# Block 0 of a fused attention and MLP kernel: when weight conversions may enter the engine queues

## Chip, cores and metric

One Trainium2 chip, one of its cores. The metric is the device time of one execution in microseconds (us). Engines: PE is TensorE, DVE VectorE, ACT ScalarE, POOL GpSimd, SP SyncE, whose queue issues all DMAs here.

## What is computed

Attention of 8 heads over 576 positions for 4 batches (4 heads see the last 32 positions, 4 heads every 32nd), then a gated layer with an RMS norm, then a second one without. All in fp32.

```python
attn_out = _attn_ref(q, k, v)                       # (4, 8, 576, 64)
x = attn_out.transpose(0, 2, 1, 3).reshape(2304, 512)
rms = np.sqrt(np.mean(x * x, axis=-1, keepdims=True) + 1e-06)
xn = x / rms * rms_g
g = xn @ w_gate                                     # 512 x 1536
x = (g * (1.0 / (1.0 + np.exp(-g))) * (xn @ w_val)) @ w_out
a, b = x @ w_a, x @ w_b
out = (a * b) @ w_out2                              # (2304, 512)
```

## The kernel before

The 2304 tokens go through the first layer in 6 blocks of 384 columns (`t`), and the hidden width of 1536 in 12 chunks of 128 (`fc`). Every fp32 operand of a product is split into a high and a low fp32r part, `hi` and `lo = x - hi`, and a product is three matmuls (`mm3`: hi·hi, hi·lo, lo·hi). For a chunk PE makes `g_ps` and `v_ps` (12 matmuls each), then `y` (12 matmuls, four accumulators that live for the block), one chunk behind. Between them, DVE multiplies `g_ps` by `rinv`, the reciprocal root mean square (line 750), ACT takes silu (751), DVE multiplies by `v_ps` to `h` (761), and `split` makes hi of h on ACT (502) and lo on POOL or DVE (503). Three PSUM slots with the tag "gv" hold g and v, so that g of chunk 2 takes the slot of v of chunk 0.

The weights come as 64-bit words, and block 0 converts them while it computes. The conversion of a third (gate, val, out; for chunks 1 to 10 gate and val go together, 1024 columns, called gv here, and out, called wo, is 512 wide) has these steps: ACT at line 134 turns the high word into a float in place; the low bits go to `cz`, either by ACT from the upper half of the low word (line 139, letter A of `LOW`) or by DVE as a shift of it (line 136, letter D); DVE joins them (line 142); ACT casts hi (147); POOL or DVE subtracts to lo (148, letters of `WLO`). A converted `wo` is also stored to DRAM (`wod`), from which later blocks load it. The raw weights of chunks 0 to 6 and some of `wo` are loaded ahead, the rest as slots become free.

Attention of block 0 runs first (list `STEPS0`); its end for this text is: `pvc` and `xstc` call `xhl` four times, which makes hi of x on ACT (384), the square on ACT (429, inside `sq`, which also issues the matmul with `ones`, 433) and lo on DVE (386). Then `rinv` takes the root on ACT (445) and the reciprocal on DVE (447). Attention of block t + 1 is spread over the chunks of block t (`attention_slot`).

The order of each engine's instructions comes from a planner of the tile framework: among the instructions that its own timeline finds ready it takes the one that was emitted first. The kernel bends this order by `tc.issue_after(i)`: within it, whatever is emitted for i's engine is queued behind i; no other engine is touched and no wait between engines is added. `gate(fc)` does so for the keys in `GATES`, each an instruction of block 0's attention: `snorm`, `sqr`, `pvr` and `rec` are on DVE, `sqrt`, `xhi` and `sexp` on ACT, `pvm` on POOL. `behind(list)` does it for a list; `made` holds h (DVE), hi (ACT) and lo of the latest chunk.

Of the kernel before, what the change touches and what calls it, by code (L numbers as in the profile page):

```python
# [10 lines left out]
F32 = mybir.dt.float32  # L11
# [4 lines left out]
ALU = mybir.AluOpType  # L16
# [9 lines left out]
NFC = FF // 128  # L26
# [17 lines left out]

GATES = ["pvm snorm sqr",
         "norm pvm snorm sqr",
         "pvr snorm xhi",
         "snorm sqr sqrt xhi",
         "rec sexp snorm sqrt xhi"]

# [14 lines left out]
WLO = ["PPP", "PPP", "PPP", "PPP", "PPP", "PPP",  # L65
       "PPP", "PPP", "PPP", "PPP", "PPP", "PPD"]

LOW = ["AAA"] * NFC
NEG = -1000000000.0
BIG = 3.0e38  # L70
SCALE = 1.0 / 8.0
# [3 lines left out]
def fused_kernel(ctx: ExitStack, tc: tile.TileContext, qtl, ktl, vl, qs, ks, vs, cst, w1, w2, out):  # L75
# [5 lines left out]
    nc = tc.nc  # L81

    def engine(c):
        return {"P": nc.gpsimd, "D": nc.vector}[c]
# [29 lines left out]
    def load_pair(w, which, pool=None):  # L114
        if pool is None:
            t = gv_slot(U32, "gv_raw")
            if which[0][1] == 0:
                gvraw[which[0][0]] = t
            return [load_raw(w, fc, k, t[:, i]) for i, (fc, k) in enumerate(which)]
        return [load_raw(w, fc, k, raw_third(pool)) for fc, k in which]  # L120
# [46 lines left out]
    def run(steps):  # L167
        for f in steps:
            f()
# [14 lines left out]
    def attention(t, pool, psum, banks):  # L184
# [4 lines left out]
        st = {}  # L189
        steps = {}  # L190

        def bank():
            return psum.tile([128, 512], F32, tag=next(banks), name="att")

        def piece(tag, name, bufs):
            return pool.tile([128, NTB], F32, tag=tag, name=name, bufs=bufs)
# [183 lines left out]
        def xhl(i, src):  # L380

            xx = act.tile([128, 2, NTB], F32R, tag="x", name="xx", bufs=8)
            hi, lo = xx[:, 0], xx[:, 1]
            st["xhi"] = nc.scalar.activation(hi, src, AF.Copy, scale=g_sb[:, i:i + 1])
            sq(i)()
            st["xlo"] = nc.vector.scalar_tensor_tensor(lo, src, g_sb[:, i:i + 1], hi.bitcast(F32), op0=ALU.mult, op1=ALU.subtract)
            xt[t, i] = xx

        def xsplit(i, src):
# [35 lines left out]
        def sq(i):  # L425
            def f():
                q_t = st["sq", i] = piece("sq", "sq", 2)
                src = st["ops" if i < 2 else "xps", i % 2][:, :NTB]
                nc.scalar.activation(q_t, src, AF.Square)
                if t == 0:  # L430
                    if i == 0:
                        st["rps"] = bank()
                    nc.tensor.matmul(st["rps"][:, :NTB], ones, q_t, start=i == 0, stop=i == 3)
                elif i:
                    engine(SQA[t]).tensor_tensor(q_t, q_t, st["sq", i - 1], op=ALU.add)
            return f
# [50 lines left out]
    def tmp(name):  # L487
        return act.tile([128, NTB], F32, tag="t", name=name, bufs=NTMP)

    made = []  # L490

    @contextmanager
    def behind(instructions):

        with ExitStack() as e:
            for i in instructions:
                e.enter_context(tc.issue_after(i))
            yield
# [17 lines left out]
    g_sb = cst_sb[:, 384:388]  # L516
# [19 lines left out]
    def load_late(which):  # L536
        raw.update(zip(which, load_pair(w1, which, pool)))

    def convert1(fc):
        t = gv[fc] = gv_slot(F32R, "gv")  # L540
        two = [raw.pop((fc, k)) for k in range(2)]
        if fc in FUSEDW:
            both, ready = gvraw[fc], t.rearrange("p k a n -> p (k a) n")
            run(conversion(both.rearrange("p k a n -> p (k a) n"), ready, pool, engine(WLO[fc][0]), LOW[fc][0]))
        else:
            run(zipped(*(conversion(two[k], t[:, k], pool, engine(WLO[fc][k]), LOW[fc][k]) for k in range(2))))

# [29 lines left out]
    @contextmanager  # L577
    def gate(fc):

        with ExitStack() as e:  # L580
            for key in GATES[min(fc, len(GATES) - 1)].split():
                e.enter_context(tc.issue_after(s0["st"][key].ins))
            yield
# [23 lines left out]
    def load_wo(t, fc):  # L607
        wt = wo[t, fc] = wo_tile()
        nc.sync.dma_start(wt.rearrange("p a n -> p (a n)").bitcast(F32), wod[fc])
# [110 lines left out]
    for t in range(NB):  # L720
        if t == 1:
            apool.close()
            pool = apool.enter_context(tc.tile_pool(name="attn", bufs=1))
        if t == NB - 1:
            apool.close()
            cpool.close()
            pool = p2.enter_context(tc.tile_pool(name="forms", bufs=1, reuse_waits="tile"))
            early = [f for k in (4, 5, 0, 1, 2, 3) for f in convert_forms(k, k < 4)]
        nxt = attention(t + 1, pool, psum, itertools.cycle(["att"])) if t + 1 < NB else None
        x = [xt[t, cc] for cc in range(NCC)]  # L730
        for fc in range(NFC):
            if t > 0 and fc == 0:
                load_wo(t, 0)
            g_ps = psum.tile([128, 512], F32, tag="gv", name="g_ps", bufs=3)
            mm_in(g_ps[:, :NTB], gv[fc], 0, x)
            v_ps = psum.tile([128, 512], F32, tag="gv", name="v_ps", bufs=3)
            mm_in(v_ps[:, :NTB], gv[fc], 1, x)
            if t == 0 and fc + 1 < NFC:
                with gate(fc + 1):
                    convert1(fc + 1)  # L740
                if fc + 2 == NFC:
                    load_late([(NFC - 2, 2), (NFC - 1, 2)])
            if t == NB - 1:
                slab[fc] = wgt.tile([128, 4 * DM], F32 if fc in (0, 1, 11) else F32R, tag="gv", name="slab", bufs=NFC)
                with behind(made):
                    run(early[len(early) * fc // NFC:len(early) * (fc + 1) // NFC])
                    for k in [k for k in x0 if k <= fc]:
                        run(x0.pop(k))
            sg = tmp("sg")
            nc.vector.tensor_tensor(sg, g_ps[:, :NTB], ri[t], op=ALU.mult)  # L750
            nc.scalar.activation(sg, sg, AF.Silu)  # L751
            if fc == 1 and t > 0:
                evac_y(t - 1)
            if nxt is not None:
                attention_slot(nxt, fc)
            if prev is not None:
                emit_y(*prev)
            if t > 0 and fc + 1 < NFC:
                load_wo(t, fc + 1)
            h = tmp("h")  # L760
            made[:] = [nc.vector.tensor_tensor(h, sg, v_ps[:, :NTB], op=ALU.mult).ins]  # L761
            hl[t, fc] = split(h, engine(HLO0[fc] if t == 0 else HLO[t]))
            if t == 0:
                wt = wo[0, fc] = wo_tile()
                with gate(fc + 1):
                    run(conversion(raw.pop((fc, 2)), wt, pool, engine(WLO[fc][2]), LOW[fc][2], True))
                nc.sync.dma_start(wod[fc], wt.rearrange("p a n -> p (a n)").bitcast(F32))
                if fc % 2:
                    load_units(1)
                if fc == NFC - 3:  # L770
                    load_late([(NFC - 1, 0), (NFC - 1, 1)])
            prev = (t, fc)
    emit_y(*prev)
    evac_y(NB - 1)
# [238 lines left out]
```

## Time and profile before

| | |
|---|---|
| median of 3 runs | 982.59 us (980.43 to 1163.71) |
| the profiled execution | 981.18 us |
| its span, first to last instruction | 979.4 us |
| mean granted clock of PE | 0.99 |
| instructions | 14348 |

The profile shows one execution. Its times count from the first instruction; the 1.8 us between its time and its span lie outside. The run of 1163.71 stands apart from the other two and from the profiled one, and is not used.

### The profile page before, as it was taken

The page shows a single profiled execution, that of the slowest core. Times are in us where ns is not written, and L with a number is a line of the kernel's source. Part 1 is how long each engine was busy: PE and PEld are TensorE (multiplying, and loading weights), DVE is VectorE, ACT ScalarE, POOL GpSimd, SP SyncE. Part 2 cuts the span into 40 slices and gives each one's busy share as a digit, 9 for nine tenths or more (in the row PEclk, how much of TensorE's full clock was granted, in tenths as well). Part 3 has the DMA queues.
Part 4 walks back from the last instruction along what each step waited for, and adds up shares of the span by engine and source line. Part 5 has one row for each costly group of instructions (what it writes and reads, how often), then busy time and mean ns, then how long its engine had stood idle before and what let it go on. Part 6 is the DMA issues. An engine that isn't in the chain of part 4 may idle for free.

```text
span 979.4 us, 14348 instructions
## 1 busy us (share of the span) xinstructions
PE 944.5 (96%) x5438; PEld 896.9 (92%) x5438; DVE 625.2 (64%) x903; ACT 429.3 (44%) x800; POOL 537.6 (55%) x406
## 2 busy tenths in 40 slices
PE   5799999999999999999998999999999999999998
PEld 4699889999999999999998999899999999999996
DVE  5578757648917885887566657666656655465534
ACT  5989645243534433433455555435335423122110
POOL 4488846558739776968346544755643424123211
PEclk7989999999999999999999999999999999999999
DMA  9953376435534553532687975897893973863701
GB/s 347 407 231 119 114 282 210 147 117 177 187 108 134 200 168 110 173 121 80 213 343 302 344 281 206 318 417 319 337 366 138 356 293 113 284 248 150 269 11 65
DMA packets 57364, 215.57 MB, mean 220 GB/s; under 512 B 5968, under 2 KB 14544, under 8 KB 51664
## 3 DMA queue, kind: packets, MB, share of 16 engines
q1 hardware_dynamic: 57296, 214.66, 59.9%
q8 instruction: 43, 0.70, 0.3%
q14 instruction: 25, 0.20, 0.1%
HBM read 172.17 MB, written 42.47 MB: 219 GB/s over the span
## 4 chain that ended last, share of the span: by engine, by line
PE 69%; DVE 10%; DMA 7%; ACT 6%; POOL 4%; issue 4%; SPq 0%; POOLq 0%; DVEq 0%; ACTq 0%
PE o L892 5%; PE o L894 5%; PE o L893 5%; PE Y L838 4%; PE Y L837 4%; PE Y L836 4%; PE y L478 3%; PE v_ps L478 3%; PE y L479 3%; PE y L480 3%; PE v_ps L480 3%; PE g_ps L478 3%; PE v_ps L479 3%; PE g_ps L480 3%; PE g_ps L479 3%
## 5 line engine op out<-in xcount | busy, mean ns | idle before, releaser
L148 POOL TENSOR_TENSOR hl<-c,hl 128x384 fp32r<-128x384 f32 x72 | 79.8, 1109 | 185.7 <-ACT hl L147 180.1
L245 POOL TENSOR_TENSOR prod<-kv_t,qs_t 128x512 f32<-128x512 f32 (+12 forms) x57 | 107.7, 1913 | 17.8 <-DMA kv_t<-in_ks 5.9
L478 PE MATMUL g_ps<-xx,gv 128*128 128x384 f32 x288 | 98.2, 341 | 5.1 <-DVE h L761 5.1
L843 DVE TENSOR_TENSOR c<-c,Y 128x384 f32<-128x384 f32 x108 | 59.3, 551 | 67.5 <-PE Y L838 59.7
L478 PE MATMUL v_ps<-xx,gv 128*128 128x384 f32 x288 | 97.7, 339 | 2.6 <-DVE sg L750 2.1
L479 PE MATMUL y<-hl,wo 128*128 128x384 f32 x288 | 96.1, 338 | 4.0 <-DVE hl L503 4.0
L479 PE MATMUL v_ps<-xx,gv 128*128 128x384 f32 x288 | 98.1, 341 | 0.0
L278 POOL TENSOR_TENSOR prod<-kv_t,S_t 128x512 f32<-128x512 f32 (+12 forms) x57 | 84.8, 1500 | 23.9 <-issue 7.4
L480 PE MATMUL v_ps<-xx,gv 128*128 128x384 f32 x288 | 97.5, 339 | 0.0
L480 PE MATMUL g_ps<-xx,gv 128*128 128x384 f32 x288 | 97.3, 338 | 0.0
L479 PE MATMUL g_ps<-xx,gv 128*128 128x384 f32 x288 | 97.1, 338 | 0.0
L480 PE MATMUL y<-hl,wo 128*128 128x384 f32 x288 | 94.8, 337 | 0.0
L503 POOL TENSOR_TENSOR hl<-h,hl 128x384 fp32r<-128x384 f32 x58 | 62.8, 1083 | 47.8 <-ACT hl L502 41.3
L281 DVE TENSOR_REDUCE xs_t<-prod 128x64 f32<-128x448 f32 (+17 forms) x57 | 85.2, 1515 | 6.0 <-POOL prod L278 5.8
L478 PE MATMUL y<-hl,wo 128*128 128x384 f32 x288 | 85.6, 343 | 1.1 <-ACT wo L147 0.9
L892 PE MATMUL o<-slab,hl 128*128 128x512 f32 x216 | 84.7, 393 | 1.0 <-DVE slab L901 0.5
L893 PE MATMUL o<-slab,hl 128*128 128x512 f32 x216 | 84.6, 392 | 0.0
L894 PE MATMUL o<-slab,hl 128*128 128x512 f32 x216 | 83.5, 395 | 0.0
L147 ACT CAST hl<-c 128x384 fp32r<-128x384 f32 x72 | 37.0, 513 | 104.1 <-DVE c L873 103.9
L751 ACT ACTIVATE sg<-sg 128x384 f32<-128x384 f32 x72 | 37.9, 526 | 90.9 <-DVE sg L750 80.3
L838 PE MATMUL Y<-slab,form 128*128 128x384 f32 x216 | 73.1, 338 | 0.0
L837 PE MATMUL Y<-slab,form 128*128 128x384 f32 x216 | 73.0, 338 | 0.0
(135 smaller groups left out, 2515.5 us busy)
## 6 DMA issues: line engine op xcount, KB each, us to landing
form<-formd SPq DMA_DIRECT2D x32, 1792.0 KB, 10.7
wo<-wod SPq DMA_DIRECT2D x60, 512.0 KB, 3.5
raw<-in_w SPq DMA_DIRECT2D x42, 512.0 KB, 6.9
gv_raw<-in_w SPq DMA_DIRECT2D x30, 512.0 KB, 10.0
formd<-form SPq DMA_DIRECT2D x6, 1792.0 KB, 6.8
formd<-forms SPq DMA_DIRECT2D x6, 1792.0 KB, 11.8
slab<-x2d SPq DMA_DIRECT2D x24, 384.0 KB, 4.5
wod<-wo SPq DMA_DIRECT2D x12, 512.0 KB, 3.3
```

Of the source, the lines that this page charges most:

```text
L148: lo_eng.tensor_tensor(lo, x, hi.bitcast(F32), op=ALU.subtract)
L245: nc.gpsimd.tensor_tensor(pr, st["ks", g][:, :, :n, :], st["qs"][:, heads(g), mm:mm + 1, :].to_broadcast([128, G, n, D]), op=ALU.mult)
L278: st["pvm"] = nc.gpsimd.tensor_tensor(pr, st["vs", g][:, :, :n, :], st["S"][:, heads(g), mm, :n, None].to_broadcast([128, G, n, D]), op=AL ...
L281: st["pvr"] = nc.vector.tensor_reduce(st["xs"][:, mm, heads(g), :], pr.rearrange("p g n d -> p g d n"), axis=X, op=ALU.add)
L478: nc.tensor.matmul(out_ps, w_hi, x_hi, start=start, stop=False)
L479: nc.tensor.matmul(out_ps, w_hi, x_lo, start=False, stop=False)
L480: nc.tensor.matmul(out_ps, w_lo, x_hi, start=False, stop=stop)
L837: nc.tensor.matmul(bank(n), hi, x[p][:, 1, c], start=False, stop=False, skip_group_check=not begins)
L838: nc.tensor.matmul(bank(n), lo, x[p][:, 0, c], start=False, stop=c == 1, skip_group_check=not begins)
L892: nc.tensor.matmul(o, h[:, 0, cols], w[0], start=n == 0, stop=False)
L893: nc.tensor.matmul(o, h[:, 0, cols], w[1], start=False, stop=False)
L894: nc.tensor.matmul(o, h[:, 1, cols], w[0], start=False, stop=n == len(chunks) - 1)
```

## The change

Four edits, all for block 0. `xhl` emits the lo part ahead of the square. The third entry of `GATES`, which holds for gv of chunk 2 (and for wo of chunk 1), names the root instead of the last reduction of the attention's products: on ACT its instructions queue behind the root, on DVE no longer behind that reduction. `wo` of chunk 0 gets the same gate (`max(fc + 1, 2)`). A list `h_made` keeps h and its two parts for each chunk of block 0; gv of chunk fc + 1 and wo of chunk fc queue, on their three engines, behind those of chunk fc - 2, which takes hold from gv 3 and wo 2 on. And the low bits of gv 1 and gv 2 are made by DVE (line 136) instead of ACT (line 139).

```diff
 GATES = ["pvm snorm sqr",
          "norm pvm snorm sqr",
-         "pvr snorm xhi",
+         "snorm sqr sqrt xhi",
          "snorm sqr sqrt xhi",
          "rec sexp snorm sqrt xhi"]
...
-LOW = ["AAA"] * NFC
+LOW = ["AAA", "DDA", "DDA"] + ["AAA"] * 9
...
             st["xhi"] = nc.scalar.activation(hi, src, AF.Copy, scale=g_sb[:, i:i + 1])
+            st["xlo"] = nc.vector.scalar_tensor_tensor(lo, src, g_sb[:, i:i + 1], hi.bitcast(F32), op0=ALU.mult, op1=ALU.subtract)
             sq(i)()
-            st["xlo"] = nc.vector.scalar_tensor_tensor(lo, src, g_sb[:, i:i + 1], hi.bitcast(F32), op0=ALU.mult, op1=ALU.subtract)
...
+    h_made = {}
     made = []
...
             if t == 0 and fc + 1 < NFC:
-                with gate(fc + 1):
+                with gate(fc + 1), behind(h_made.get(fc - 2, [])):
                     convert1(fc + 1)
...
                 wt = wo[0, fc] = wo_tile()
-                with gate(fc + 1):
+                with gate(max(fc + 1, 2)), behind(h_made.get(fc - 2, [])):
                     run(conversion(raw.pop((fc, 2)), wt, pool, engine(WLO[fc][2]), LOW[fc][2], True))
...
+            if t == 0:
+                h_made[fc] = list(made)
             prev = (t, fc)
```

## Rows read from the trace of the kernel before

**Rows 1.** The page, part 1: busy us, share of the span, instructions.
```profile
PE 944.5 (96%) x5438; PEld 896.9 (92%) x5438; DVE 625.2 (64%) x903; ACT 429.3 (44%) x800; POOL 537.6 (55%) x406
```
**Rows 2.** Stretches: length, busy us (instructions) by engine, PE's clock, DMA share, GB/s.
```profile
33.40:56.20 22.80, 17.10 (x79) 15.92 (x78) 12.16 (x14) 22.30 (x32) 10.61 (x6) 0.85 1.04 407
56.20:126.90 70.70, 67.93 (x432) 63.89 (x430) 56.66 (x68) 56.60 (x111) 61.24 (x40) 1.00 0.38 138
126.90:180.00 53.10, 49.74 (x303) 48.26 (x304) 36.37 (x63) 24.59 (x61) 33.18 (x30) 1.00 0.65 225
180.00:979.40 799.40, 787.38 (x4470) 750.24 (x4468) 502.57 (x720) 304.67 (x554) 416.89 (x316) 1.00 0.59 216
```
**Rows 3.** Waits of PE, 33 to 260 us: us in total, times, longest.
```profile
PE g_ps L478 <- DVE h L761: 5.1, 2, 4.7
```
**Rows 4.** Timeline of PE: start, us, instruction, tiles, count, idle before and releaser.
```profile
33.48 0.42 PE L478 MATMUL g_ps<-xx,gv 128*128 128x384 f32 x1
...
44.29 0.34 PE L480 MATMUL v_ps<-xx,gv 128*128 128x384 f32 x1
49.37 0.69 PE L478 MATMUL g_ps<-xx,gv 128*128 128x384 f32 x1 [4.75 <-DVE h L761]
...
56.23 0.85 PE L478 MATMUL y<-hl,wo 128*128 128x384 f32 x4
56.92 0.34 PE L478 MATMUL g_ps<-xx,gv 128*128 128x384 f32 x1
...
59.00 0.34 PE L478 MATMUL v_ps<-xx,gv 128*128 128x384 f32 x1
```
**Rows 5.** Timeline of ACT, 31 to 49 us.
```profile
31.52 1.16 ACT L134 ACTIVATE gv_raw<-gv_raw 128x1024 f32<-128x1024 f32 x1
32.55 1.15 ACT L139 ACTIVATE cz<-gv_raw 128x1024 uint32<-128x1024 uint16 x1
33.56 0.69 ACT L134 ACTIVATE gv_raw<-gv_raw 128x512 f32<-128x512 f32 x1
...
34.67 0.90 ACT L429 ACTIVATE sq<-att 128x384 f32<-128x384 f32 x2
...
37.50 0.58 ACT L445 ACTIVATE rms_t<-att,eps_sb 128x384 f32<-128x384 f32 x1 [0.47 <-PE att L433]
...
46.91 1.28 ACT L751 ACT_TABLE_LOAD   x1
48.20 0.52 ACT L751 ACTIVATE sg<-sg 128x384 f32<-128x384 f32 x1
```
**Rows 6.** Timeline of DVE, 38 to 49 us.
```profile
38.12 2.55 DVE L447 RECIPROCAL rinv<-rms_t 128x384 f32<-128x384 f32 x1 [1.51 <-ACT rms_t L445]
...
41.66 0.55 DVE L750 TENSOR_TENSOR sg<-g_ps,rinv 128x384 f32<-128x384 f32 x1
42.77 1.23 DVE L142 SCALAR_TENSOR_TENSOR cz<-gv_raw,cz 128x1024 uint32<-128x1024 uint32 x1 [0.56 <-ACT cz L139]
...
48.76 0.56 DVE L761 TENSOR_TENSOR h<-sg,v_ps 128x384 f32<-128x384 f32 x1 [3.62 <-ACT sg L751]
```
**Rows 7.** Timeline of POOL: lo parts of gv 3, wo 2, h 0 and gv 7.
```profile
46.97 2.35 POOL L148 TENSOR_TENSOR gv<-cz,gv 128x1024 fp32r<-128x1024 f32 x1 [6.73 <-ACT gv L147]
...
52.09 1.28 POOL L148 TENSOR_TENSOR wo<-cz,wo 128x512 fp32r<-128x512 f32 x1
53.33 1.02 POOL L503 TENSOR_TENSOR hl<-h,hl 128x384 fp32r<-128x384 f32 x1
...
75.36 2.39 POOL L148 TENSOR_TENSOR gv<-cz,gv 128x1024 fp32r<-128x1024 f32 x1
```
**Rows 8.** Line 343 up to 137 us: duration ns min/median/max, first and last start, forms.
```profile
L343 DVE TENSOR_SCALAR lsm<-lsm x6: 153/658/1329, 11.6 to 80.8; 128x4 f32<-128x4 f32 x4, 64x8 f32<-64x8 f32 x2
```
**Rows 9.** Timeline of ACT: first step of gv 7, and hi of h 4.
```profile
65.70 1.13 ACT L134 ACTIVATE gv_raw<-gv_raw 128x1024 f32<-128x1024 f32 x1
...
80.72 0.50 ACT L502 CAST hl<-h 128x384 fp32r<-128x384 f32 x1
```

## Prediction

> **What bounds the kernel now.** Read the page first: TensorE (PE) is busy for 96% of the span [rows 1], so a change elsewhere pays only where PE stands still or runs slowly. Then the stretches, one row for each: of the 799 us behind 180 us PE is busy for 787, so nothing is to be won there except that all of it starts earlier. Block 0's run-up, 33.4 to 56.2, is the bad one: 17.10 busy of 22.80, at a mean granted clock of 0.85, that is partly at the lower of the two levels (1.2 instead of 2.4 GHz), while ScalarE (ACT) is busy for 22.30 [rows 2]. Third, the waits of PE: of the 5.1 us spent on h (VectorE, line 761), one wait has 4.7 [rows 3]. Fourth, the timelines around that wait. PE issues the last matmul of v_ps 1 at 44.29 and the first of g_ps 2 at 49.37; from there to the end of chunk 2 at 56.23 it needs 6.86 us for 24 matmuls, against 2.08 us for 12 in chunk 3 (59.00 - 56.92), 0.173 us each [rows 4]. PE waits for a PSUM slot: three hold g and v, and g_ps 2 takes that of v_ps 0, which is free after h 0.
>
> Following h 0 back: it ran at 48.76, right behind silu 0 (48.20, after a table load at 46.91), whose input sg was there at 41.66 + 0.55 = 42.21 [rows 5, 6]. So silu 0 stood 6.0 us in ACT's queue behind conversions. The sg itself waited for the reciprocal (38.12, 2.55 us), this for the root at 37.50, this for the last two squares at 34.67, and those stood behind four conversion steps that ACT took from 31.52 on [rows 5, 6]. These are the two queues that the change touches.
>
> **The change, part by part.** *Ahead of the root.* The conversions of gv 2, wo 0 and wo 1 move behind it; the four steps from 31.52 to 34.67 go, 3.15 us [rows 5]. The low bits of gv 1 (one ACT step, as 1.15 us of gv 2) leave ACT as well; some half microsecond of that helps, since the products that feed x 0 bound it next. I take the root 3.6 us earlier, at 33.9 (bounds 3.0 and 5.0). Reciprocal: 34.5 to 37.1. In the kernel before, a conversion step stood between it and sg 0; I keep none, so sg 0 is made at 37.65, 4.6 us earlier, if g_ps 0 is through: 12 matmuls from 33.48 end at 35.6 [rows 4].
>
> *The lo parts ahead of the squares.* VectorE (DVE) and ACT are different engines, so this only lets the four lo parts precede other DVE work; matmuls of g_ps 0 with lo need them. DVE has gaps there; I set it at nothing, bounds -0.6 and +0.6 us.
>
> *Silu 0 and h 0.* Between root and silu 0, ACT may now find only gv 2, wo 0 and wo 1. Their first two steps (1.16 for gv 2; some 0.69 each for four wo steps, by the one at 33.56 [rows 5]) make 3.9 us, a little more than the 3.25 us from the end of the root (34.4) to sg. They end at 38.3; with the table load of 1.28 silu 0 starts near 39.6 and h 0 is done near 40.7 (0.52 and 0.56 us [rows 5, 6]); if the three closing casts (1.1 + 2 x 0.69) slip in front too, near 43.2. Before: 49.3. So 6 to 9 us earlier.
>
> *gv 2 as the next to be late.* Its chain now begins at the root: ACT 34.4 to 35.6; the shift on DVE behind reciprocal and sg, near 37.7. No row shows this shift. Nearest from above is line 142 over the same 1024 words, 1.23 us [rows 6]; from below half of it, 0.6; I take 1.2, the same width on the same engine. Then line 142, 1.23, to 40.1, the cast 1.1, to 41.2, the lo part on GpSimd (POOL) 2.35 [rows 7], to 43.6. PE is done with g 0, v 0, g 1 and v 1 (48 matmuls, 8.3 us) at 41.8, starts g_ps 2 at once and waits for lo parts to about 43. Chunk 2 ends near 47.2 at the full clock, against 56.23: **9 us ahead**. Of that some 6.3 is the earlier start and 2.7 the clock (6.86 - 24 x 0.173).
>
> A wait that the shift adds, first from the row: TENSOR_SCALAR on DVE, line 343, takes 153 ns at best and 1329 ns at worst for the same few elements [rows 8], the long ones beside busy POOL. The Trainium skill, page "SBUF — State Buffer", section "Who interferes with whom", says why it can speak against this change: tensor_scalar in a two-port mode, and an operation with two SBUF inputs, share a port pair with GpSimd as an exclusive lock, so low bits on DVE could block on POOL's instructions where ACT's never do. By that rule the sum would lose up to one POOL conversion, 2.35 us, on gv 2 and nothing on gv 1; by the best row nothing. The trace agrees with the lock. POOL has little to do at 36 to 40, so I leave it at nothing, with 1.2 us in the range.
>
> *Behind the root: the three-chunk rule.* From gv 3 and wo 2 on, each conversion queues on ACT, DVE and POOL behind h, hi and lo of three chunks before (gv) or two (wo). What is queued behind these waits are L134, L139, L142, the casts and POOL's lo parts, and for them wait PE and, on SP's queue, the stores wod<-wo and the loads behind them. The price is the run-ahead: before, ACT converted through gv 6 while PE stood still. Sum it for the stretch from the end of chunk 2 to the start of block 1 (70.7 us, 56.2 to 126.9 [rows 2]). POOL: 61.24 busy, and to it come what was done before 56.2 and now falls behind 47.2: lo parts of gv 3 and gv 4 (2 x 2.35), wo 2 (1.28), h 0 (1.02): 68.2 us [rows 2, 7]. ACT: 56.60, and what is left over: before, it worked 56.2 - 38.0 = 18.2 us without a gap behind the root; now 47.2 - 34.4 = 12.8, of which the moved gv 2 and wo 0, wo 1 take 2.3 + 6 x 0.69 = 6.4; so 11.8 us are left over: 68.4. PE: 67.9. All three need 68 us, so from 47.2 the stretch can't end before 115.6. Before, PE filled 67.93 of 70.70 (96%) and POOL 87%. Three engines that are all full, tied by short waits, will not each reach 96%; I take 91.5%, between the two rows: 68.4 / 0.915 = 74.8, block 1 starts at **122.0 instead of 126.9, 4.9 us earlier**. So 4 of the 9 us are given back. At 96% it is 118.5 (8.4 gained), at 87% 125.8 (1.1 gained).
>
> *Behind 127 us.* Block 2's attention loads queue on SP behind the last wo store, so they move with block 0's conversions; PE stands for 3.4 of 53.1 us there and 12 of 799 afterwards [rows 2], which I keep.
>
> **Sum.** The profiled execution took 981.18 (span 979.4 and 1.8 around it); it lies between the two undisturbed runs shown, 980.43 and 982.59, the latter being the median. 981.2 - 4.9 = 976.3, so **976**.
>
> **Rivals.** *Absorbed (980).* The wait on h 0 turns into the same time lost later, since ACT and POOL have no spare. For it: the equal sums of 68 us and POOL's 87%. Against: PE's share was 96% although POOL and DVE were full there. 981.2 - 1.1 = 980. The same time comes out if the planned order leaves silu 0 behind the casts and gv 2 late, which is the case that the change doesn't do what it says.
>
> *Slower: the rule starves PE (986).* The loop is: hi of h(k-3) on ACT, conversion of gv k, matmuls of chunk k, silu and h k. gv 7's conversion took from 65.70 to 75.36 + 2.39 = 77.75, 12.05 us, and started 15 us before the split of h 4 (80.72) that it must now follow [rows 7, 9]. Matmuls 4.2. The end of v to the split took about 7 us there, as the split stood behind exponentials of the next block's attention. That makes 23.3 us for three chunks, 7.8 each, hardly under the 70.7 / 9 = 7.9 of before. From 47.2 the break-even is (126.9 - 47.2) / 9 = 8.9 a chunk, 26.6 a loop. If fuller queues stretch the conversion from 12 to 15 and the split from 7 to 9, the loop is 28.2, the stretch 84.6, and block 1 starts at 131.8: 4.9 us later, 986. Against it: silu and split come sooner when fewer conversions stand ahead of them.
>
> *More than forecast (970).* At 96% in block 0, 8.4 us are kept, and PE's 3.4 us behind 127 shrink: 981.2 - 8.4 - 2.5 = 970.
>
> **How the numbers follow.** Forecast (973 to 978.5) 0.45; absorbed (to 982.5) 0.22; slower 0.20; more 0.13. The range that leaves out a third of the last two, and takes in the bounds above (root 1.4, shift 1.2, casts in front 2.5 us), is 968 to 986. A measurement of this kernel tells about 2%, some 20 us, from no change: that is more than all that PE loses between 33 and 180 us (5.7 + 2.8 + 3.4 idle [rows 2] and 2.7 by the clock, 14.6). So faster by over 2% 0.02, slower 0.04, within 0.94.
>
> **What would show it.** The root near 34 and no conversion of gv 2, wo 0 or wo 1 ahead of it on ACT; silu 0 near 39.6; no 4.7 us wait of PE for h, a granted clock of 1.00 from 33 to 56; line 136 on DVE near 1.2 us; chunk 2 done near 47; block 1 beginning at 122; POOL and ACT above 90% between. Wrong if gv conversions (line 148) end after PE wants them, seen as PE waits for ACT's gv cast in chunks 4 to 9, or if the order of later blocks, planned anew, moves by more than the sum.

## The result, and the profile after

| | before | after |
|---|---|---|
| median | 982.59 us (980.43 to 1163.71, 5 runs) | 991.23 us (988.44 to 994.18, 5 runs) |
| the profiled execution | 981.18 us | 988.44 us |
| its span | 979.4 us | 986.3 us |

The ratio is 1.0095, interval 1.0076 to 1.0113: the changed kernel is slower by about 9 us. That is clear of no change, and less than the 2% at which the prediction would have called it slower. 976 was forecast, and 986 was the upper end of the range. The run of 1163.71 stands apart from the other four of its kernel and is not used.

The stretches of after come first, cut as in [rows 2]: length, busy us (instructions) of PE, its weight loads, DVE, ACT and POOL, granted clock of PE, DMA share, GB/s.

```profile
33.40:56.20 22.80, 20.04 (x110) 18.56 (x109) 11.58 (x14) 17.90 (x26) 11.48 (x7) 1.00 1.01 389
56.20:126.90 70.70, 61.04 (x368) 55.76 (x367) 54.81 (x65) 59.06 (x111) 60.98 (x39) 0.95 0.30 110
126.90:180.00 53.10, 49.80 (x293) 48.50 (x292) 33.85 (x61) 26.83 (x65) 32.47 (x28) 0.97 0.75 262
180.00:986.30 806.30, 794.06 (x4509) 756.24 (x4508) 508.60 (x726) 305.80 (x557) 421.48 (x320) 1.00 0.59 214
```

The run-up did get better: 110 matmuls against 79, clock 1.00 against 0.85. The next stretch lost more than that: 368 matmuls against 432. Behind 180 us PE stands still for 12 us, as before. So block 0 decides, and a table of progress shows where in it. For each n it has the start of the matmul behind the first n of the 384-wide matmuls of g, v and y (36 belong to a chunk), worked out from the timelines of PE:

```
n        before   after   after - before
 48       49.37   45.60   -3.8
 72       56.23   49.99   -6.2
144       70.49   64.38   -6.1
192       80.98   75.82   -5.2
216       86.03   83.97   -2.1
288      101.76  101.78    0.0
336      112.18  114.26   +2.1
360      118.42  124.20   +5.8
408      128.79  138.56   +9.8
600      169.52  176.52   +7.0
2500     538.33  545.73   +7.4
```

Three things happen: a lead of 6.2 us is made by n = 72 (the end of g and v of chunk 2 in the kernel before; here four of the 72 are of y already); it is gone by n = 288; and 9.8 us are lost in the last chunks, of which 7 stay to the end.

The tables and times below compare single profiled executions, and these differ before any edit plays a part. Up to the first matmuls of line 354 the instructions on PE, ACT, DVE and POOL are the same, in the same order, in all twenty kernels; yet the first of them starts at 14.48 in before, 13.77 in after and 14.85 to 16.28 in the others. So 0.7 us of after's lead was there from the start, and a difference of 1 or 2 us between two traces is not by itself the work of an edit.

**The start.** The timeline of ACT around the root, with what replaces [rows 5]:

```profile
29.02 0.49 ACT L429 ACTIVATE sq<-att 128x384 f32<-128x384 f32 x1
...
29.86 0.51 ACT L429 ACTIVATE sq<-att 128x384 f32<-128x384 f32 x1
31.08 0.49 ACT L429 ACTIVATE sq<-att 128x384 f32<-128x384 f32 x1 [0.71 <-PE att L433]
32.38 0.49 ACT L429 ACTIVATE sq<-att 128x384 f32<-128x384 f32 x1 [0.81 <-PE att L433]
37.20 0.58 ACT L445 ACTIVATE rms_t<-att,eps_sb 128x384 f32<-128x384 f32 x1 [4.32 <-PE att L433]
37.68 0.66 ACT L134 ACTIVATE gv_raw<-gv_raw 128x512 f32<-128x512 f32 x1
38.24 0.65 ACT L139 ACTIVATE cz<-gv_raw 128x512 uint32<-128x512 uint16 x1
38.79 1.66 ACT L134 ACTIVATE gv_raw<-gv_raw 128x1024 f32<-128x1024 f32 x2
40.95 0.62 ACT L147 CAST wo<-cz 128x512 fp32r<-128x512 f32 x1 [0.50 <-DVE cz L142]
42.07 1.05 ACT L147 CAST gv<-cz 128x1024 fp32r<-128x1024 f32 x1 [0.51 <-DVE cz L142]
43.14 1.28 ACT L752 ACT_TABLE_LOAD   x1
44.43 0.53 ACT L752 ACTIVATE sg<-sg 128x384 f32<-128x384 f32 x1
```

The conversions are gone from ahead of the root, the squares end at 32.9 and not at 35.6, and still the root runs at 37.20, 0.3 us earlier than before, which is less than the two traces differ at their start. ACT stands idle for 4.32 us and waits for a matmul of line 433. Why that is late is to be seen in the order of PE's matmuls:

```profile
31.54 0.81 PE L433 MATMUL att<-sq,ones 128*128 128x384 f32 x2
32.18 0.71 PE L560 MATMUL idle<-ones 128*128 128x256 bf16 x5
32.65 0.42 PE L478 MATMUL g_ps<-xx,gv 128*128 128x384 f32 x1
...
34.82 0.81 PE L433 MATMUL att<-sq,ones 128*128 128x384 f32 x2
35.17 0.63 PE L478 MATMUL v_ps<-xx,gv 128*128 128x384 f32 x1
...
36.35 0.81 PE L433 MATMUL att<-sq,ones 128*128 128x384 f32 x2
...
45.60 0.44 PE L478 MATMUL g_ps<-xx,gv 128*128 128x384 f32 x1 [0.68 <-DVE h L762]
```

The matmuls of the third and fourth square stand behind all 12 matmuls of g_ps 0 and five of v_ps 0. The squares have two buffers, so the third and fourth also wait for PE (0.71 and 0.81 us above).

**The middle.** The waits of PE from 56.2 to 118 us: in total, times, longest. None is as long as the 4.7 us of [rows 3], but there are five of them, all for conversions or h. In the kernel before, PE waits in this stretch for the attention (line 281, 1.3 us) and twice for `wo` (0.9).

```profile
PE g_ps L480 <- POOL gv L148: 2.8, 2, 1.6
PE g_ps L478 <- DVE h L762: 2.3, 1, 2.3
PE y L478 <- ACT wo L147: 0.9, 2, 0.6
```

**The end of block 0.** ACT's casts of the last `wo` and the steps of chunk 11's weights (the 512-wide raw and gv), on ACT's timeline:

```profile
122.10 0.67 ACT L139 ACTIVATE cz<-raw 128x512 uint32<-128x512 uint16 x1
...
123.53 0.62 ACT L147 CAST wo<-cz 128x512 fp32r<-128x512 f32 x1 [0.36 <-DVE cz L142]
...
126.34 0.67 ACT L139 ACTIVATE cz<-raw 128x512 uint32<-128x512 uint16 x1
...
129.20 0.62 ACT L147 CAST wo<-cz 128x512 fp32r<-128x512 f32 x1 [0.88 <-DVE cz L142]
129.80 0.62 ACT L147 CAST gv<-cz 128x512 fp32r<-128x512 f32 x1
132.74 0.67 ACT L134 ACTIVATE raw<-raw 128x512 f32<-128x512 f32 x1 [2.33 <-DMA raw<-in_w]
...
134.58 0.66 ACT L134 ACTIVATE raw<-raw 128x512 f32<-128x512 f32 x1 [0.62 <-DMA raw<-in_w]
```

and the loads of raw words on SP's queue, of after and then of before:

```profile
123.52 0.33 SPq L108 DMA_DIRECT2D raw<-in_w  x1
...
129.20 0.93 SPq L108 DMA_DIRECT2D raw<-in_w  x2
```

```profile
113.36 0.33 SPq L108 DMA_DIRECT2D raw<-in_w  x1
...
118.94 1.40 SPq L108 DMA_DIRECT2D raw<-in_w  x2
```

Chunk 11's gate and val are loaded into the two raw slots that wo 8 and wo 9 hold. wo 8's slot is free when its join on DVE (line 142) is done, at 123.5; its lo part frees the one `cz` buffer that all of `wo` shares; then come wo 9's low bits (126.34, behind the table load and root of block 1's attention on ACT), its join (128.54, behind the reciprocal of that attention on DVE), and at 129.20 the load for the second half of chunk 11. That lands as ACT resumes, and PE gets v_ps 11 going at 136.34 and block 1 at 136.8, 9.9 us later than before. Both ends of this chain are 10 us later: 123.5 against 113.4 at its head. PE also waits for wo 9 itself, 2.33 us, until its cast of 129.20 lets y of chunk 9 begin at 129.87.

### The profile page after: what moved, and what is told of

Same layout as the page of the kernel before. It is cut to its first block, busy times and chain, and to the rows that moved or that the text cites. A ratio compares the mean times of both kernels' runs of the same rounds, so it can differ in the third digit from the quotient of the medians.

```text
span 986.3 us, 14355 instructions
## 1 busy us (share of the span) xinstructions
PE 950.0 (96%) x5438; PEld 900.1 (91%) x5438; DVE 628.0 (64%) x905; ACT 427.1 (43%) x798; POOL 540.4 (55%) x406
## 4 chain that ended last, share of the span: by engine, by line
PE 70%; DVE 9%; DMA 6%; ACT 6%; issue 4%; POOL 3%; SPq 0%; POOLq 0%; ACTq 0%; DVEq 0%
PE o L895 5%; PE o L897 5%; PE o L896 5%; PE Y L841 4%; PE Y L840 4%; PE Y L839 4%; PE v_ps L478 3%; PE y L478 3%; PE y L479 3%; PE v_ps L480 3%; PE y L480 3%; DMA gv_raw<-in_w 3%; PE v_ps L479 3%; PE g_ps L480 3%; PE g_ps L478 3%
## 5 line engine op out<-in xcount | busy, mean ns | idle before, releaser
L479 PE MATMUL y<-hl,wo 128*128 128x384 f32 x288 | 98.9, 345 | 4.0 <-DVE hl L504 4.0
L480 PE MATMUL y<-hl,wo 128*128 128x384 f32 x288 | 93.5, 336 | 0.0
L478 PE MATMUL y<-hl,wo 128*128 128x384 f32 x288 | 90.0, 351 | 3.4 <-ACT wo L147 3.2
L504 POOL TENSOR_TENSOR hl<-h,hl 128x384 fp32r<-128x384 f32 x58 | 65.7, 1133 | 47.0 <-ACT hl L503 40.6
L752 ACT ACTIVATE sg<-sg 128x384 f32<-128x384 f32 x72 | 37.7, 524 | 91.5 <-DVE sg L751 82.0
```

Source lines behind the costliest of these rows:

```text
L478: nc.tensor.matmul(out_ps, w_hi, x_hi, start=start, stop=False)
L479: nc.tensor.matmul(out_ps, w_hi, x_lo, start=False, stop=False)
L480: nc.tensor.matmul(out_ps, w_lo, x_hi, start=False, stop=stop)
```

## The experiments

Each ran beside the kernel before; the ratio is to that. The theories that the expectations name: ROOT, the lead is too small because the root is late; GATE and RULE, the new gate or the three-chunk rule cause the loss; ORDER, the planner puts matmuls ahead of the squares' matmuls; BACKLOG, the work that ACT and POOL did not do ahead of silu 0 comes back in chunks 4 to 8; TAIL, the time is set by when wo 8 and wo 9 free the raw slots for chunk 11; ROW, the row of `wo` conversions with its one buffer started too late.

**Parts of the change.** `no_rule` is the changed kernel without `behind(h_made...)`; `gate_alone` and `rule_alone` are the kernel before with only the gates, or only the rule; `lo_and_low` is it with the lo parts ahead of the squares and the two D letters; `lo_alone` with the lo parts alone.

```diff
 no_rule (after)
-                with gate(max(fc + 1, 2)), behind(h_made.get(fc - 2, [])):
+                with gate(max(fc + 1, 2)):
...
-                with gate(fc + 1), behind(h_made.get(fc - 2, [])):
+                with gate(fc + 1):
 gate_alone (before)
-         "pvr snorm xhi",
+         "snorm sqr sqrt xhi",
...
-                with gate(fc + 1):
+                with gate(max(fc + 1, 2)):
 lo_alone (before)
-            sq(i)()
             st["xlo"] = nc.vector.scalar_tensor_tensor(lo, src, g_sb[:, i:i + 1], hi.bitcast(F32), op0=ALU.mult, op1=ALU.subtract)
+            sq(i)()
```

> The changed kernel without the three-chunk rule (no behind(h_made) at either place); gate, lo order and low bits as changed. Theory RULE (conversions that must queue behind h of three chunks before start too late, so PE waits for lo of gv and for wo in chunks 4 to 9, and wo 8 and wo 9 free their raw buffers 10 us late): the loss in chunks 4 to 11 goes and the 6 us won by chunk 3 stay, 975 to 978. Theory GATE (the root came only 0.3 us earlier, at 37.2, while ACT stood idle for 5.8 us and POOL for 11 us ahead of it; the work put off there comes back later): still 986 to 992.

> The kernel before with the gate edits alone (gv 2, wo 0 and wo 1 behind the root). Theory RULE: 976 to 982, an earlier silu 0 and nothing lost later. Theory GATE: 986 to 992, the lost ACT and POOL time comes back in chunks 4 to 11.

> The kernel before with the three-chunk rule alone (h_made and behind at both places). Theory RULE: silu 0 comes near 42 and PE's 4.7 us wait goes, but chunks 4 to 11 lose more: 985 to 992. Theory GATE: the rule is harmless and the wait for h 0 goes: 974 to 980.

> The kernel before with the lo parts ahead of the squares and the low bits of gv 1 and gv 2 on DVE, no gate, no rule. Both theories: within 2 us of the kernel before, 980 to 984; line 136 takes 0.7 us alone and up to 1.75 us beside POOL. If neither edit is neutral, a third theory is needed.

> The kernel before with the lo parts ahead of the squares, nothing else. ORDER (the planner then puts g and v matmuls ahead of the squares' matmuls, and the root waits for them): root at 40 us or later on ACT against 37.50, time 986 to 990. COVERED (the lo parts lie in gaps of DVE, as the prediction had it): root within 0.6 us of 37.50, time 980 to 984.

Measured: no_rule 993.99 us (1.0112, 1.0088 to 1.0135), gate_alone 988.98 (1.0059, 1.0044 to 1.0074), rule_alone 992.20 (1.0096, 1.0074 to 1.0119), lo_and_low 988.32 (1.005, 1.0033 to 1.0067), lo_alone 993.06 (1.01, 1.0063 to 1.0137). So no single part carries the loss: each costs 5 to 11 us alone, and all together cost 9. GATE had the time of gate_alone and RULE nearly that of rule_alone; neither had the other's, no_rule came out above both, and both had 980 to 984 for lo_and_low. The two D letters alone were not run. The parts lose it in different places. rule_alone leads by 8.1 us at n = 168, more than the whole change, and is 9.7 late at 408. gate_alone has silu 0 at 48.6 and no_rule at 50.5, no earlier than before: without the rule the planner puts the conversions of gv 3 and more of wo ahead of silu 0. The rule is what makes the early silu 0.

The lo parts were costed at nothing. The timeline of ACT in lo_alone:

```profile
38.41 0.49 ACT L429 ACTIVATE sq<-att 128x384 f32<-128x384 f32 x1 [0.44 <-PE att L433]
42.48 0.58 ACT L445 ACTIVATE rms_t<-att,eps_sb 128x384 f32<-128x384 f32 x1 [3.58 <-PE att L433]
```

Root at 42.48, 5.0 us later than before, by this one swap of two lines (4.1 us by the table below): ORDER, though the time is worse than it had given (986 to 990). With lo made first, the matmuls of g 0, v 0 and g 1 become ready before the last squares' matmuls, and stand ahead of them in PE's queue.

**The start mended.** `four_squares` gives the squares of block 0 four buffers (from a tag that has them); `squares_first` puts `sq(i)()` ahead of the lo part again; `before_four_squares` is the first edit on the kernel before.

```diff
 four_squares, before_four_squares
-                q_t = st["sq", i] = piece("sq", "sq", 2)
+                q_t = st["sq", i] = tmp("sq") if t == 0 else piece("sq", "sq", 2)
```

> The changed kernel with a buffer of its own for each of the four squares of block 0 (they take the tag t of sg and h instead of two buffers of their own). Theory ROOT (the root stays at 37 us because the matmuls of squares 2 and 3 stand behind those of g_ps and v_ps in PE's queue; square 2 has to wait for the buffer of square 0): the four matmuls of squares come ahead of g_ps, the root moves to 33 or 34, h 0 to 41, and the 4 us stay to the end, 984 to 986. Theory TAIL (the end of block 0 is set by the row of wo conversions, one cz buffer for all, whose 8th and 9th free the buffers for the raw words of chunk 11): an earlier root moves the start, yet block 1 starts 9 to 10 us late all the same, 987 to 991.

> The changed kernel with the squares ahead of the lo parts again. Theory ROOT: lo parts ahead let the planner put g_ps and v_ps ahead of the last two matmuls of squares; with squares ahead they come 2 to 3 us sooner, root 34 to 35, and the total gains as much, 985 to 987. Theory TAIL: 987 to 991.

> The kernel before with four buffers for the squares of block 0. If squares wait for buffers in the kernel before too, the root comes some 1 to 2 us earlier than 37.50. FREE LEAD: the time falls by as much, 980 to 982. TAIL (any shift of the wo conversions relative to the raw words of chunk 11 costs more than the start gives): 984 to 990.

Measured: four_squares 992.93 (1.0093, 1.0074 to 1.0112), squares_first 990.62 (1.0071, 1.0055 to 1.0087), before_four_squares 985.97 (1.0033, 1.002 to 1.0047). In four_squares the root is at 35.17 and silu 0 at 42.40, and the lead is 9.4 us at n = 168, which is what the prediction had wanted. It is +4.8 at 240 and +11.7 at 408 all the same. A better start does not reach block 1. In squares_first the root comes at 38.08: the last square's matmul still stands behind nine matmuls of g_ps 0. In before_four_squares the squares end at 33.5, but the planner uses the gap for the same conversions and two casts as before, and the root comes at 38.28.

As the traces differ at their start, the root is better counted from the first matmul of line 354:

```
kernel               line 354   root    apart
before                 14.48    37.50    23.0
after                  13.77    37.20    23.4
gate_alone             16.28    37.22    20.9
lo_alone               15.39    42.48    27.1
squares_first          15.77    38.08    22.3
four_squares           15.14    35.17    20.0
before_four_squares    15.52    38.28    22.8
wo_as_before           15.04    41.22    26.2
```

So the gates alone do bring the root 2.1 us closer, and the change as a whole puts it 0.4 us further off. The lo order costs 4.1 us in the kernel before, but going back on it in the changed one gains only 1.1; the two buffers for the squares cost 3.4 us there, and next to nothing in the kernel before.

**The tail.** `changed_no_gv11` and `before_no_gv11` leave chunk 11's gate and val out: they are neither loaded nor converted, and chunk 11 computes with those of chunk 10. `changed_cz2`, `before_cz2` and `four_squares_cz2` give `wo` two `cz` buffers and pay for them with one of the four pieces of `x_t`.

```diff
 no_gv11
-                    convert1(fc + 1)
+                    if fc + 2 == NFC:
+                        gv[fc + 1] = gv[fc]
+                    else:
+                        convert1(fc + 1)
...
-                if fc == NFC - 3:
-                    load_late([(NFC - 1, 0), (NFC - 1, 1)])
 cz2
-NCZ = {False: 2, True: 1}
+NCZ = {False: 2, True: 2}
-piece("xr", "x_t", 4)
+piece("xr", "x_t", 3)
```

> The changed kernel without the weights of chunk 11: gate and val of chunk 11 are not loaded and not converted, its matmuls use those of chunk 10. Theory TAIL: block 1 starts 8 to 10 us earlier than in the changed kernel (126 to 129 instead of 136.8), 979 to 983 in all. Theory STARVED (PE lacks converted weights all through chunks 4 to 11, by the three-chunk rule and the late conversions): 2 us less than the changed kernel at most, for the two conversions left out, 986 to 990.

> The kernel before without the weights of chunk 11, the same edit. Both theories: 0 to 3 us under the kernel before, 979 to 983, since PE waits little for chunk 11 there (its waits around 126 us are 0.5 us).

> The changed kernel with two cz buffers for wo conversions instead of one (and three instead of four x_t pieces in attention, which makes the room). Theory TAIL (one buffer makes the twelve wo conversions a row, and its 8th and 9th link hold up the raw words of chunk 11): the first of the loads at 123.5 comes 4 to 8 us earlier, 982 to 986. Theory BACKLOG (ACT lost 8 us of idle time ahead of silu 0, so everything that ACT, DVE and POOL do for block 0 ends late, buffers or not): the loads come at 121 or later, 988 to 992.

> The kernel before with the same two cz buffers. Theory TAIL: the load at 113.4 comes a little earlier and chunk 11 with it, 979 to 983. Theory BACKLOG: no more than 2 us either way, 981 to 985, unless the new plan upsets the order.

> The changed kernel with four square buffers and two cz buffers. Theory TAIL: the early start of the one (9 us ahead at chunk 4) and the shorter row of the other add up, 978 to 984. Theory BACKLOG: 988 to 993 as with four squares alone.

Measured: changed_no_gv11 979.99 (0.9965, 0.9952 to 0.9979), before_no_gv11 975.92 (0.9924, 0.9909 to 0.9939): the same cut takes 11.2 us from the changed kernel and some 7 from the one before (where both theories had 0 to 3), and what the change costs shrinks from 8.6 to 4.1 us by the medians. In the profiled executions, of which that of changed_no_gv11 is the fastest of its nine runs, it is less still: progress of changed_no_gv11 equals that of after up to n = 312, within 0.5 us, and is +0.1 at 408 where after is +9.8; block 1 begins at 128.2 in it and at 128.1 in before_no_gv11, and the spans are 974.5 and 973.7. What remains of the 4.1 us lies in runs that have no trace in this study. In the kernel before, block 1 starts no earlier by the cut (128.1 against 126.9): its gain lies behind block 0. So loading and converting chunk 11's words holds up block 1 in the changed kernel, by 8.6 us, and not in the one before.

changed_cz2 984.52 (1.0028, 1.0015 to 1.0041), before_cz2 986.37 (1.0042, 1.0029 to 1.0056), four_squares_cz2 984.79 (1.0031, 1.002 to 1.0041). The second buffer, with the piece of `x_t` that pays for it, takes 6.7 us from the changed kernel and costs the one before some 4, more than either theory had; no run separates the two edits. In changed_cz2 the raw words for chunk 11 come from 102.68 on, 21 us earlier, and block 1 starts 4.3 us earlier:

```profile
102.68 0.33 SPq L108 DMA_DIRECT2D raw<-in_w  x1
...
113.76 7.85 SPq L108 DMA_DIRECT2D raw<-in_w  x3
```

A table shows how tight the link is, with the start of wo 8's cast on ACT and of block 1's first matmul, read from the timelines of these kernels and of those told further below:

```
kernel                      wo 8   block 1   apart
before                     113.4     126.9    13.5
after                      123.5     136.8    13.3
no_rule                    127.1     140.5    13.5
gate_alone                 124.7     138.6    13.9
rule_alone                 123.0     136.8    13.8
lo_and_low                 121.4     134.8    13.3
lo_alone                   124.9     144.9    20.0
four_squares               124.4     137.4    13.0
squares_first              125.3     138.7    13.3
before_four_squares        119.7     133.5    13.7
wo_as_before               129.5     141.9    12.4
low_bits_7                 129.0     142.2    13.2
changed_cz2                103.9     132.5    28.6
before_cz2                 109.1     137.6    28.5
four_squares_cz2           106.0     133.6    27.6
four_squares_cz2_no_rule   107.0     136.0    29.0
changed_cz2_no_rule        108.7     139.7    30.9
four_squares_cz2_low_7     108.7     134.9    26.2
changed_no_gv11            121.8     128.2     6.3
before_no_gv11             114.0     128.1    14.1
```

With one buffer and chunk 11's words block 1 starts 12.4 to 13.9 us behind wo 8 in eleven of twelve kernels, while wo 8 itself moves by 16 us; with two buffers the distance doubles. The even distance is a sign and no proof: before_no_gv11 has 14.1 without those words. In lo_alone PE itself is late: it works through g, v and y without a wait from 131 to 142 us. What shows the link in the changed kernel is the cut above, and the load at 123.52, issued as wo 8's join ends (122.80 + 0.69). In four_squares_cz2 block 1's attention then ends last: on PE the rest of v_ps 11 stands behind one of its matmuls, and on DVE h of chunk 11 stands behind a memset for block 2's attention that waits for another (line 441). The two rows, from PE's timeline and from DVE's:

```profile
128.58 0.33 PE L409 MATMUL att<-cst_sb,xs_t 128*128 128x128 f32 x1 [2.42 <-DVE xs_t L281]
```

```profile
132.88 0.24 DVE L227 MEMSET S_t<- 128x216 f32 x1 [2.38 <-PE att L441]
133.04 0.49 DVE L762 TENSOR_TENSOR h<-sg,v_ps 128x384 f32<-128x384 f32 x1
```

**The row started early.** `wo_as_before` is the changed kernel with the gates of wo 0 and wo 1 as before.

```diff
-    def gate(fc):
+    def gate(fc, wo=False):
...
-            for key in GATES[min(fc, len(GATES) - 1)].split():
+            for key in ("pvr snorm xhi" if wo and fc == 2 else GATES[min(fc, len(GATES) - 1)]).split():
...
-                with gate(max(fc + 1, 2)), behind(h_made.get(fc - 2, [])):
+                with gate(fc + 1, True), behind(h_made.get(fc - 2, [])):
```

> The changed kernel with the gates of before for wo 0 and wo 1 alone (they may run ahead of the root; gv 2, the three-chunk rule, lo order and low bits as changed). Theory TAIL: the row of wo starts 12 to 17 us earlier, and block 1 starts 4 to 9 us earlier, 981 to 986. Theory BACKLOG: ACT fills some 4 us of its idle time ahead of silu 0, and the total gains 3 to 4 us, 986 to 988. If the row is paced by POOL's queue later on, its early start is lost by wo 5 and nothing changes, 989 to 992.

Measured: 997.37 (1.0155, 1.0139 to 1.0171). wo 0 is cast at 24.6 and wo 1 at 34.7, as early as before, but wo 8 at 129.5, the latest of all. The root comes late in it too (41.22, 26.2 us behind line 354), so its time alone would not settle the matter. But ROW falls: the head of the row does not set its end. In rule_alone and lo_alone too wo 0 comes at 25 and wo 8 at 123 to 125. The row is paced on the way, and by what is open.

**The middle.** `four_squares_cz2_no_rule` and `changed_cz2_no_rule` take the rule out with the tail mended; `low_bits_7` and `four_squares_cz2_low_7` leave the rule and take four steps of 1.13 us from ACT, by letter D for gv 4 to gv 7.

```diff
-LOW = ["AAA", "DDA", "DDA"] + ["AAA"] * 9
+LOW = ["AAA", "DDA", "DDA", "AAA", "DDA", "DDA", "DDA", "DDA"] + ["AAA"] * 4
```

> The changed kernel with four buffers for the squares of block 0 and two cz buffers for wo, now without the three-chunk rule. RULE (the rule eats the lead of 10.5 us between the 168th and the 240th matmul of block 0): at least 5 us of the lead are left at the 240th, and the time is 976 to 980. BACKLOG (ACT and POOL have the work left over whatever the queueing): the lead is gone by the 240th to 300th as with the rule, time 983 to 987.

> The changed kernel with two cz buffers for wo and without the three-chunk rule. RULE: better than the 984.5 us with the rule by 3 us or more, 978 to 981. BACKLOG: 983 to 987, as with the rule.

> The changed kernel with the low bits of gv 4 to gv 7 by VectorE too, so that ACT has 4 x 1.13 = 4.5 us less to do in the stretch from 60 to 100 us where it was busy for 39.5 of 40. BACKLOG (ACT's work left over eats the lead): the 240th matmul of block 0 is 3 us or more earlier than in the changed kernel (lead 4 us or more instead of 1.1); with the tail unmended the time falls by 1 to 4, 987 to 990. RULE (the loop of three chunks eats it): the loop gets shorter by no more than the difference of a step on ACT and on VectorE, so the lead at the 240th stays within 1 us of 1.1 and the time within 2 us of 991.

> The changed kernel with four buffers for the squares of block 0, two cz buffers for wo, and the low bits of gv 4 to gv 7 by VectorE too. BACKLOG: of the lead of 10.5 us at the 168th matmul at least 4 are left at the 240th, and block 1 begins at 129 or earlier instead of 133.6; time 978 to 982, level with the kernel before or under it. RULE: lead at the 240th within 1.5 us of 0.4, time 983 to 987.

Measured: four_squares_cz2_no_rule 986.77 (1.0045, 1.0028 to 1.0062), changed_cz2_no_rule 991.29 (1.0083, 1.0068 to 1.0098), low_bits_7 997.85 (1.0147, 1.0124 to 1.017), four_squares_cz2_low_7 986.60 (1.0038, 1.0021 to 1.0056). Without the rule there is no lead to eat: silu 0 is at 47.3 in the first, against 41.5 with it, and n = 168 is 1.3 us ahead and not 10.5. So RULE, as the expectations had it, is wrong: taking it out costs 2 to 7 us, in changed_cz2_no_rule more than either theory gave.

BACKLOG was drawn from the stretches 60:80 and 80:100, of before and then of after:

```profile
60.00:80.00 20.00, 20.00 (x135) 19.67 (x134) 17.78 (x23) 17.17 (x43) 20.00 (x12) 1.00 0.28 100
80.00:100.00 20.00, 19.39 (x133) 18.32 (x132) 16.75 (x20) 18.54 (x31) 17.13 (x12) 1.00 0.35 126
```

```profile
60.00:80.00 20.00, 18.15 (x118) 17.18 (x117) 17.39 (x24) 19.70 (x49) 20.00 (x13) 1.00 0.35 125
80.00:100.00 20.00, 17.67 (x107) 16.68 (x106) 12.59 (x20) 19.83 (x30) 14.61 (x10) 0.91 0.31 109
```

ACT is busy for 39.5 of 40 us, against 35.7 before: the work that it didn't do while it waited for the root (24.0 us busy between 24 and 56.2, against 31.3) has come back. That alone is not what holds PE. The same two stretches in low_bits_7:

```profile
60.00:80.00 20.00, 16.62 (x105) 15.27 (x103) 19.49 (x23) 13.78 (x31) 16.69 (x11) 1.00 0.36 121
80.00:100.00 20.00, 15.69 (x95) 14.89 (x96) 14.81 (x22) 17.27 (x36) 13.84 (x9) 0.91 0.20 69
```

ACT is busy for 8.5 us less there (4.5 of them were taken from it) and the lead is lost sooner, at n = 192 (+0.6), and the time is 6.6 us worse than after. From 60 to 80 us DVE is now the full engine (19.49 of 20). Neither theory had given that time. In four_squares_cz2_low_7 the lead is 4.3 us at 240, as BACKLOG said, and lost by 288; block 1 begins at 134.9 and not at 129, and the time is not the 978 to 982 that BACKLOG gave with it. So a full ACT alone does not explain the give-back; nor was a version found that keeps a lead. In after one instance can be read in full: gv 6 was let in by the split of h 3 (64.58 on ACT), its first step follows at 64.98, its lo part ends at 77.85 on POOL, and PE waits for it until 77.90, 1.23 us. That is the loop of the rule, 12.9 us from the first step to the weights. Whether such loops or the order of short steps in three full queues eat the most is open; no run separates the two.

The trace of after shows where the 5.2 us between n = 192 and 288 went: 25.96 us against 20.78 for as many matmuls, of which PE stood still for 2.9 more and was busy for 2.2 more, at a granted clock of 0.93 against 1.00. The still time is the 1.23 us above and the one long wait, 2.33 us for h, until 83.97. On DVE that h stands behind a join of 512 words that took 2.30 us, where one beside an idle POOL took 0.69 (134.00); POOL was busy with line 245 from 80.55 to 82.81. DVE's timeline:

```profile
81.06 2.30 DVE L142 SCALAR_TENSOR_TENSOR cz<-gv_raw,cz 128x512 uint32<-128x512 uint32 x1
83.29 0.54 DVE L762 TENSOR_TENSOR h<-sg,v_ps 128x384 f32<-128x384 f32 x1
```

Behind the wait the clock is 0.50 from 86 to 88 us. No run takes this wait out, so what it is worth in the end is not shown.

## Why the prediction was wrong

By its own steps, on the profiled executions: forecast -9.0 + 4.1 = -4.9 us; measured -6.2, then +6.2, then +9.8, then -2.5 in block 1, together +7.3 (988.44 - 981.18).

- *Root 3.6 us earlier.* **This step failed first.** Measured 0.3, and 0.4 later when counted from line 354, though ACT's conversions left as foreseen. The sum followed ACT alone; the root waited 4.32 us for the matmul of the fourth square, which PE took behind 17 matmuls of g and v. The gates and four buffers together did make it early (four_squares, 3.0 us by the same count); four buffers on the kernel before did not.
- *Lo parts ahead of the squares: nothing, bounds ±0.6.* Only DVE and ACT were looked at. The emission order is also PE's order, and g and v matmuls went ahead of the squares' matmuls. Alone on the kernel before that costs 4 to 5 us on the root (lo_alone); in the changed kernel it is one cause of two, beside the two buffers, as squares_first shows.
- *Silu 0 at 39.6, to 44.4.* Of the 4.8 us, 3.3 are the root and 1.5 come behind it, where the closing casts of wo 0 and gv 2 did slip in front of it, as the prediction had as its second case. h 0 at 45.0 and gv 2's last part (until 45.6) came level, so PE began g_ps 2 at 45.60.
- *9 us ahead at the end of chunk 2.* 6.2. The clock's part came, at a granted clock of 1.00: 4.39 us for 24 matmuls, from 45.60 to 49.99, where 4.15 were reckoned and 6.86 were needed before. What is missing is the start: PE was to begin at 41.8 and be held by lo parts to some 43; it began at 45.60, when h 0 had freed its slot and the lo part of gv 2 was done.
- *Low bits on DVE, 1.2, port lock up to 2.35 on gv 2, nothing on gv 1.* The other way round, and small; rows below.
- *The stretch from chunk 2 to block 1: 68.4 us of work at 91.5%, 74.8 us.* **This is the step that decided the sign.** From 49.99 to 136.80 it took 86.8. The work itself came near the sum (ACT 71.2 us, POOL 70.5, PE 74.3, partly at the lower clock), so it is the share of it in the stretch that was wrong: 81 to 86%. The two parts of the stretch differ, as these rows show (columns as in [rows 2]):

```profile
49.99:101.78 51.79, 47.61 (x298) 45.13 (x298) 39.02 (x52) 50.85 (x94) 45.11 (x27) 0.97 0.43 158
101.78:136.80 35.02, 26.69 (x136) 23.10 (x136) 23.74 (x23) 20.38 (x37) 25.39 (x19) 0.90 0.31 113
```

- *Its first part, to n = 288.* ACT is full (50.85 of 51.79) and all 6.2 us were given back, where four of nine were foreseen. That is the rival "absorbed" at this point. The equal sums of 68 us were right as a warning, but low_bits_7 shows that moving work off ACT does not remove the loss. The trace shows one wait for h and the lower clock behind it as most of it; no run tests that.
- *Its second part, to block 1.* No engine is full, so a sum of work could not show it. The prediction followed chunks, and not the row of `wo` beside them, which came 10 us late to wo 8 in the changed kernel; no single gate or rule was found to cause that, as each part alone delays it too (121.4 to 124.9). Chunk 11's words hang on wo 8 and wo 9, and the sum had no line for that. In the profiled executions it is worth 9.7 of the 9.8 us at 408 (changed_no_gv11 has +0.1 there); by the medians the cut takes away 4.5 of the 8.6 us that the change costs. Why the row comes late is open.
- *Behind 127 us, nothing.* That held: the loss there fell, from 9.8 to 7.4 us.
- *The slower rival (986, block 1 at 131.8)* had the sign and nearly the size, by another mechanism: PE starved for gv all through, by the loop of three chunks. Waits for gv add up to only 2.8 us from 56 to 118 us; it is gv of chunk 11 that came late, by its raw slots.
- *"The order of later blocks, planned anew, moves by more than the sum"* was named as what could make it wrong. Something of the kind was seen in block 0 itself: each of the 18 kernels of the experiments came out slower than the kernel before, but for the two that leave out chunk 11's gate and val. That a new order costs time as such is not shown by it.

## What to carry to other kernels

When two lines of emission are swapped, look at every engine on which either enables work: the swap was between ACT and DVE, and the price was paid in PE's queue. When traces of two kernels are compared by the clock, compare first something that no edit can have touched. When work is queued later, list for each of its buffers who is waiting for the release, down to the loads of the last chunk; a lead that PE had in the middle was worth nothing here, where a row of conversions with one buffer decided when the last weights arrived. And a lead has to be followed to the end of the stage before it is counted.

## What the runs showed of the hardware

The shift on DVE (line 136, 1024 words), alone, is faster than line 142 over as many words (0.69 us against 1.22), and it took longer beside POOL. The timeline of DVE in after:

```profile
24.02 1.75 DVE L136 TENSOR_SCALAR cz<-gv_raw 128x1024 uint32<-128x1024 uint32 x1
25.87 1.22 DVE L142 SCALAR_TENSOR_TENSOR cz<-gv_raw,cz 128x1024 uint32<-128x1024 uint32 x1
27.02 0.69 DVE L136 TENSOR_SCALAR cz<-gv_raw 128x1024 uint32<-128x1024 uint32 x1
```

The first stood beside a POOL conversion (23.95, 1.27 us), the second beside none: 1.06 us apart. In squares_first, too, it takes 1.75 us beside POOL and 0.69 without. The Trainium skill, page "SBUF — State Buffer", section "Who interferes with whom", has the one that comes second block for the whole instruction of the other, and by that the first could lose up to what is left of the POOL instruction, 1.20 us here; the trace agrees. The forecast had put this price on gv 2; both shifts ran ahead of the root, and gv 1 paid it.

The clock that the earlier silu 0 gave back in the run-up (1.00 against 0.85) was lost again where PE had waited: 0.91 from 80 to 100 us, with 0.50, the level of 1.2 GHz, from 86 to 88, behind the wait of 2.33 us that ended at 83.97; and 0.84 from 118 to 140, where PE stood still for 6.4 of 22 us:

```profile
118.00:140.00 22.00, 15.56 (x66) 13.67 (x66) 10.08 (x12) 14.13 (x23) 11.83 (x10) 0.84 0.46 167
```
